# Attention with a Mish MLP: the second-mask value products as quarter tiles, with the sums of a pair in two PSUM banks

## The chip, the cores and the metric

One core of a Trainium2 chip runs the whole kernel. The metric is the device time of one execution in microseconds, the median of three runs. One execution was also profiled; its trace is what the rows below come from. TensorE does the matrix products, VectorE, ScalarE and GpSimd the elementwise work, and SyncE (SP) issues the DMAs. In the views they are PE (PEld for its weight loads), DVE, ACT, POOL and SP.

## What is computed

Eight batches, eight heads, 576 positions, head size 64, all in fp32. Attention is causal with a window of 128 keys; its output, laid out as 4608 rows of 512, goes through an MLP with a Mish activation.

```python
scores = scale * np.matmul(q, k.transpose(0, 1, 3, 2))
rel = pos[:, None] - pos[None, :]
mask = (rel >= 0) & (rel < 128)
scores = np.where(mask, scores + bias, -1e9)
attn = np.exp(scores - scores.max(-1)); attn = attn / (attn.sum(-1) + 1e-9)
x = np.matmul(attn, v)                    # (8, 8, 576, 64) -> (4608, 512)
h = x @ w_in                              # 512 -> 2048
g = h * np.tanh(np.log1p(np.exp(h)))
out = g @ w_out                           # 2048 -> 512
```

## The kernel before

**The MLP.** Batches are taken one after another, 512 positions each; the last 64 positions of all batches are collected in DRAM (`xs`) and form a ninth group. For each group `first` (line 756) does the products with `w_in` into PSUM tiles `h`, `mish` the activation, `parts` (line 778) splits the result into a high and a low part, and `second` (line 810) does the products with `w_out` into `po`. High and low parts make three products of reduced-precision fp32 out of one exact one. ScalarE makes the high part by a copy and the low part is the difference; for the activations GpSimd subtracts, for x VectorE does (`x_high`, `x_low`, lines 320 to 326).

**The attention.** Heads are taken in pairs (`p` = 0 to 3), one head on array columns 0 to 63, the other on 64 to 127. The first 512 queries of a pair are two half pairs (`unit`, line 328, `half` = 0 and 1) of 256 queries, two blocks of 128 each; the last 64 queries of both heads go together (`last_unit`, line 458). A group of 64 queries sees at most 192 keys: 64 old ones, 64 middle ones that are all in reach, and 64 new ones. The steps of a half pair:

- `scores`: products of queries and keys as quarter tiles of the array (64 rows by 64 columns), four at a time, into two PSUM banks (`s`).
- `exps`: VectorE adds the bias and takes the extreme (`pz`, `mx`), ScalarE the exponential and the sum (`sm`).
- `fold`, `scale`: old and new keys of one query never share a place in the mask, so the new ones are added onto the old ones, and 128 weights remain instead of 192; all are divided by the sum.
- `weights`: TensorE transposes the 128 weights; VectorE multiplies them out of PSUM with two masks (`masks`), so that two versions lie side by side in `pz`.
- `values`: products with the values. The first-mask version is taken with `va`, the second with `vs`, values shifted by 64 positions, or the other way round; all of them over 128 array rows, both heads side by side, into one PSUM bank `o` for both halves of a pair.
- `split_x`: `x_high` and `x_low` of the whole 512 columns.

The last queries' transposes and sums share another bank, tag `w` (`st["t"]`, `pt_0l` to `pt_3l` in the trace), copied out as `xo` and sent to `xs`. The x of pairs 0 to 2 takes the buffers in which their values lie (`load_v`, line 291), so it can be written only when the value products are done.

**The order.** TensorE and SP run in the order in which the program issues; a hand-written list of due times (`times`, lines 447 and 521) says where each step of the attention lies between the products of `second` of the batch before (line 913). VectorE, ScalarE and GpSimd are ordered by a planner, except in the stages marked fixed. From batch 2 on (`b > 1`), the value products of both halves and of the last queries of a pair follow each other, then come the last queries' scores and the two halves' scores of the next pair, in one slot; the transposes of both halves come in two steps some ten products of `second` later. In batch 1 each half has its slot of its own, and GpSimd folds and scales. Batch 0 runs by itself at the start (`first_attention`) while the weights come in.

Of the kernel before, what the change touches and what calls it, by code (L numbers as in the profile page):

```python
# [60 lines left out]
def attention_mish_mlp(  # L61
# [47 lines left out]
    vb = [const.tile([P, P], F32, tag=f"vb{i}", name=f"vb{i}") for i in range(2)]  # L109
    for t in vb:  # L110
        nc.gpsimd.memset(t[64:P], 0.0)


    masks = const.tile([P, 2, P], BF16, tag="masks", name="masks")
    nc.gpsimd.memset(masks, 1.0)
    for r in (slice(0, 64), slice(64, P)):

        nc.gpsimd.affine_select(
            out=masks[:, 0, r], in_=masks[:, 0, r], compare_op=ALU.is_gt, fill=0.0, base=0,
            pattern=[[-1, 64]], channel_multiplier=1,  # L120
        )
        nc.gpsimd.affine_select(
            out=masks[:, 1, r], in_=masks[:, 1, r], compare_op=ALU.is_ge, fill=0.0, base=0,
            pattern=[[1, 64]], channel_multiplier=-1,
        )
# [165 lines left out]
    def load_v(b, p):  # L291
        cs = slice(p * P, (p + 1) * P)

        pl, tag = (xp, f"x{p}") if p < NP - 1 else (at, "v")
        t = pl.tile([P, 2, 4, P], F32, tag=tag, name=f"v{b}_{p}", bufs=1)
        va, vs = t[:, 0], t[:, 1]
        load(va, v[b, 0:CH, cs].rearrange("(k p) d -> p k d", p=P))
        load(vs, v[b, 64:S, cs].rearrange("(k p) d -> p k d", p=P))
        load(vb[p % 2][:64], v[b, CH:S, cs])
        qkv[("v", b, p)] = ((va, vs), vb[p % 2])  # L300
# [19 lines left out]
    def x_high(b, p, o):  # L320
        x = xt[(b, p)] = xp.tile([P, 2, CH], F32R, tag=f"x{p}", name=f"x{b}_{p}")
        act.activation(x[:, 0, :], o, AF.Copy)

    def x_low(b, p, o):
        x = xt[(b, p)]
        dve.tensor_tensor(out=x[:, 1, :], in0=o, in1=x[:, 0, :].bitcast(F32), op=ALU.subtract)

    def unit(b, p, half):
# [8 lines left out]
        name = f"{b}_{p}_{half}"  # L337

# [28 lines left out]
        def fold():  # L367
            sm, pz = st["sm"], st["pz"]
            if b == 1:
                two = pz if half else pz[:, 1:4:2]  # L370
                pool.tensor_tensor(out=two[:, :, :64], in0=two[:, :, :64], in1=two[:, :, P:SPAN], op=ALU.add)
            act.activation(sm, sm, AF.Copy, bias=1e-9)
            dve.reciprocal(sm, sm)

        def scale():
            sm, pz = st["sm"], st["pz"]
            if b == 1:
                pool.tensor_tensor(
                    out=pz[:, :, :P], in0=pz[:, :, :P],
                    in1=sm.rearrange("p (c n) -> p c n", n=1).to_broadcast([P, 4, P]), op=ALU.mult,  # L380
                )
                return

            unread = at.tile([P, 4], F32, tag="un", name=f"un{name}")
            for c in range(4):
                n = 0
                if half or c % 2:
                    n = 64
                    dve.tensor_tensor_reduce(
                        out=pz[:, c, :n], in0=pz[:, c, :n], in1=pz[:, c, P:SPAN], scale=sm[:, c : c + 1],  # L390
                        scalar=3.0e38, op0=ALU.add, op1=ALU.min, accum_out=unread[:, c : c + 1],
                    )
                act.activation(pz[:, c, n:P], pz[:, c, n:P], AF.Copy, scale=sm[:, c : c + 1])

        def weights():
# [3 lines left out]
            for c in range(4):  # L399
                pe.transpose(pt[:, c, :], pz[:, c, :P], ident)  # L400
            if half == 0:
# [7 lines left out]
                in1=masks.rearrange("p u (c n) -> p u c n", c=1).to_broadcast([P, 2, n, P]),  # L409
# [12 lines left out]
        def pieces(t, c0, count, step):  # L422
            if step == 64:
                return t[:, c0 : c0 + 64 * count]
            return t.rearrange("p (k n) -> p k n", n=64)[:, c0 // 64 : (c0 + step * (count - 1)) // 64 + 1 : step // 64, :]

        def values():
            va = qkv[("v", b, p)][0]
            if half == 0:
                qkv[("o", b, p)] = ps.tile([P, 512], F32, tag="o", name=f"o{b}_{p}")  # L430
            o = qkv[("o", b, p)]
            for n, (vu, kb, c0, count, step, oc) in enumerate(prods):
                for i in range(2):
                    pf = st["pz"][:, 2 * i : 2 * i + 2, :].rearrange("p a n -> p (a n)")
                    pe.matmul(
                        pieces(o[HEAD[i]], oc, count, step), lhsT=va[vu][:, kb, HEAD[i]],
                        rhs=pieces(pf, c0, count, step),
                        start=(half == 0 and n == 0), stop=(half == 1 and n == len(prods) - 1),
                        skip_group_check=True,
                    )  # L440
# [13 lines left out]
        return list(zip(times, (  # L454
            scores, lambda: exps(0), lambda: exps(1), fold, scale, weights, values, split_x,
        )))

    def last_unit(b, p):
# [27 lines left out]
        def fold():  # L486
# [3 lines left out]
            un = at.tile([P, 1], F32, tag="unl", name=f"un{name}")  # L490
# [6 lines left out]
        def weights():  # L497
            t = st["t"] = ps.tile([P, 512], F32, tag="w", name=f"pt{name}")
# [5 lines left out]
                in1=masks[:, :, :64].rearrange("p u (i n) -> p u i n", i=1).to_broadcast(shape),  # L504
# [3 lines left out]
        def values():  # L508
            va, vl = qkv[("v", b, p)]
            o = st["t"][:, P : P + LEFT]  # L510
            for n, val in enumerate((va[0][:, 3, :], vl)):
                for i in range(2):
                    pe.matmul(
                        o[HEAD[i]], lhsT=val[:, HEAD[i]], rhs=st["pf"][:, n, i, :],
                        start=(n == 0), stop=(n == 1), skip_group_check=True,
                    )
# [4 lines left out]
        times = (-0.001, 0.5, 0.9, 1.4, 1.995)  # L521
        if b > 1:
            times = (-0.01, 0.21, 0.5, 1.78 if p == 1 else 1.7, 1.98)
        return list(zip(times, (scores, exps, fold, weights, values)))
# [458 lines left out]
```

## Time and profile before

| what | value |
|---|---|
| median of three runs | 975.83 us (974.78 to 976.23) |
| span of the profiled execution | 973.1 us |
| instructions in the trace | 17500 |
| TensorE matmul busy | 962.8 us, 99%, 6660 records |
| TensorE weight loads busy | 788.4 us, 81% |
| VectorE, ScalarE, GpSimd busy | 351.9 us (36%), 454.4 us (47%), 260.1 us (27%) |
| traffic to and from HBM | 56.49 MB read, 10.49 MB written, 69 GB/s |

The span runs from the first to the last instruction; what lies around it is the rest of the device time. Matmul records overlap, since each is shown from its start to its last result, so what one costs is read from the distance of starts rather than from its own duration. Every fp32 product of the attention is two passes, and each pass is one record. Times in the rows are microseconds from the start of the span, with two decimals.

### The profile page before, as it was taken

What the parts mean: (1) busy time and instruction counts of PE and PEld (TensorE: products, weight loads), DVE (VectorE), ACT (ScalarE), POOL (GpSimd) and SP (SyncE); (2) the same over time, 40 slices, a digit from 0 to 9 for tenths busy, and PEclk for the clock granted to TensorE, in tenths of its full rate; (3) what the DMA queues carried; (4) which work ended last, traced back from release to release, by engine and by line L of the source; (5) the groups of instructions that cost most, each with busy time, mean ns of one, the idle gap of its engine ahead of it and who ended that gap; (6) DMA issues with size and microseconds to landing.
All of it is one profiled execution on the core that took longest, in us unless ns stands there. A gap on an engine that the chain in (4) does not pass through costs nothing.

```text
span 973.1 us, 17500 instructions
## 1 busy us (share of the span) xinstructions
PE 962.8 (99%) x6660; PEld 788.4 (81%) x6660; DVE 351.9 (36%) x1430; ACT 454.4 (47%) x1256; POOL 260.1 (27%) x238
## 2 busy tenths in 40 slices
PE   9899999999999999999999999999999999999998
PEld 7688778888888888888888888888888888888886
DVE  5896861056302660066203750166105640100000
ACT  6798753165425653276315742366316642322121
POOL 5578751023111221032102311032102311241042
PEclk9999999999999999999999999999999999999999
DMA  7993320032102410123002410222003210000001
GB/s 200 357 371 102 98 81 22 1 108 89 50 1 73 120 32 23 46 76 100 24 1 73 123 51 0 73 74 77 24 1 103 69 45 1 22 22 23 1 12 32
DMA packets 70244, 68.12 MB, mean 70 GB/s; under 512 B 14480, under 2 KB 50960, under 8 KB 70160
## 3 DMA queue, kind: packets, MB, share of 16 engines
q1 hardware_dynamic: 69744, 66.67, 21.7%
q8 instruction: 53, 0.87, 0.4%
q10 hardware_dynamic: 416, 0.33, 0.1%
q14 instruction: 31, 0.25, 0.1%
HBM read 56.49 MB, written 10.49 MB: 69 GB/s over the span
## 4 chain that ended last, share of the span: by engine, by line
PE 89%; DMA 5%; POOL 2%; SPq 1%; issue 1%; DVE 1%; ACT 0%; POOLq 0%
PE po L49 39%; PE h L49 36%; PE s L49 8%; PE o L49 5%; DMA wi<-in_moe_w_in_dram 2%; DMA wo<-in_moe_w_out_dram 2%; POOL so L49 1%; SPq L49 1%; POOL gg L49 1%; DVE pz L49 1%; PE warm L49 1%; PE pt_0l L49 0%; DMA qk<-in_k_dram 0%; PE pt_2l L49 0%; PE pt_1l L49 0%
## 5 line engine op out<-in xcount | busy, mean ns | idle before, releaser
L49 PE MATMUL po<-so,gg 128*128 128x512 f32 x1728 | 420.8, 396 | 0.0
L49 PE MATMUL h<-x,si 128*128 128x512 f32 x1728 | 393.3, 389 | 0.0
L49 PEld LDWEIGHTS h<-x,si 128*128 128x128 f32 x1728 | 324.2, 188 | 67.4
L49 PEld LDWEIGHTS po<-so,gg 128*128 128x128 f32 x1728 | 317.0, 188 | 71.7 <-issue 8.9
L49 POOL TENSOR_TENSOR gg<-g,gg 128x512 fp32r<-128x512 f32 x144 | 186.2, 1294 | 653.6 <-ACT gg L49 653.5
L49 DVE CUSTOM_DVE_ANT_0 pz<-s,nb 128x192 f32<-128x192 f32 (+1 forms) x308 | 92.1, 328 | 299.5 <-PE s L49 296.9
L49 ACT ACTIVATE g<-h 128x1024 f32<-128x1024 f32 x72 | 74.1, 1030 | 255.5 <-PE h L49 255.5
L49 ACT ACTIVATE pz<-pz,mx 128x192 f32<-128x192 f32 (+1 forms) x256 | 110.9, 434 | 42.1 <-DVE mx L49 40.2
L49 ACT ACTIVATE gg<-g 128x512 fp32r<-128x512 f32 x144 | 89.8, 625 | 73.0 <-PE po L49 69.2
L49 DVE COPY ob<-po 128x512 f32<-128x512 f32 x18 | 12.3, 686 | 126.0 <-PE po L49 126.0
L49 PEld LDWEIGHTS o<-pz,v 128*64 128x64 f32 x1120 | 45.7, 137 | 13.2 <-DVE pz L49 8.5
L49 ACT ACTIVATE x<-o 128x512 fp32r<-128x512 f32 x32 | 19.1, 596 | 79.1 <-PE o L49 34.9
L49 DVE CUSTOM_DVE_ANT_0 pz<-pz,sm 128x64 f32<-128x64 f32 x144 | 55.5, 433 | 1.3
L49 DVE TENSOR_TENSOR pz<-s,masks 128x512 f32<-128x512 f32 (+1 forms) x56 | 52.5, 946 | 4.7 <-PE s L49 4.7
L49 ACT ACTIVATE pz<-pz,sm 128x128 f32<-128x128 f32 (+1 forms) x192 | 53.2, 348 | 0.1
L49 PE MATMUL o<-pz,v 128*64 128x64 f32 (+2 forms) x1120 | 51.2, 245 | 0.1
L49 ACT ACTIVATION_READ_ACCUMULATOR pz<-pz,mx 128x1 f32 x256 | 47.8, 187 | 0.0
L49 PE MATMUL s<-ident,pz 128*128 128x128 f32 (+1 forms) x280 | 41.4, 274 | 0.9 <-POOL pz L49 0.9
L49 PEld LDWEIGHTS s<-ident,pz 128*128 128x128 f32 (+1 forms) x280 | 33.6, 138 | 9.9 <-POOL pz L49 1.8
L49 PE MATMUL s<-qk 64*64 64x192 f32 (+1 forms) x896 | 40.8, 316 | 0.0
L49 ACT ACTIVATE ob<-po 128x512 f32<-128x512 f32 x18 | 10.8, 598 | 52.0 <-PE po L49 52.0
L49 PEld LDWEIGHTS s<-qk 64*64 64x64 f32 x896 | 28.7, 132 | 4.8 <-issue 0.4
(159 smaller groups left out, 528.2 us busy)
## 6 DMA issues: line engine op xcount, KB each, us to landing
v<-in_v_dram SPq DMA_DIRECT2D x56, 256.0 KB, 3.7
wi<-in_moe_w_in_dram SPq DMA_DIRECT2D x16, 512.0 KB, 10.7
wo<-in_moe_w_out_dram SPq DMA_DIRECT2D x16, 512.0 KB, 10.2
out_dram<-ob SPq DMA_DIRECT2D x32, 256.0 KB, 2.0
qk<-in_q_dram SPq DMA_DIRECT2D x28, 288.0 KB, 3.1
qk<-in_k_dram SPq DMA_DIRECT2D x28, 288.0 KB, 3.6
first<-in_v_dram SPq DMA_DIRECT2D x4, 256.0 KB, 3.8
vs<-in_v_dram SPq DMA_DIRECT2D x4, 256.0 KB, 3.8
```

The source lines that it names most:

```text
L49: ins = method(*args, **kwargs)
```

## The change

The half pairs keep their 128 folded weights, but in the second half the fold now lies behind the middle keys: the new keys' place takes the sum (`both`), and the weights that are transposed are columns 64 to 191 (`folded`). So in the first half the keys that need the second mask lie in array rows 0 to 63, in the second half in rows 64 to 127. The mask tile has a third plane for that. Products with the first version stay over 128 rows. Products with the second version, whose other half would be zeros, are taken over their 64 rows only, as quarter tiles; so is the last queries' product with `vl`, for which `vb` shrinks to 64 rows. They are kept in `late` and issued together by `late_values`, one of the first half (rows 0 to 63) after one of the second (rows 64 to 127), for both heads. The first half's sums go into the last queries' bank, the second half's into `o`, so the two row halves write to different banks. x is split in two pieces of 256 columns. From batch 2 on the late products of a pair come right behind the next pair's last-query scores; in batch 1 each half has its own late step.

```diff
-    masks = const.tile([P, 2, P], BF16, tag="masks", name="masks")
+    vb = [const.tile([64, P], F32, tag=f"vb{i}", name=f"vb{i}") for i in range(2)]
+    masks = const.tile([P, 3, P], BF16, tag="masks", name="masks")
     nc.gpsimd.memset(masks, 1.0)
+    for plane, base, sign, op in ((0, 0, 1, ALU.is_gt), (1, 0, -1, ALU.is_ge), (2, 64, -1, ALU.is_ge)):
+        for r in (slice(0, 64), slice(64, P)):
+            nc.gpsimd.affine_select(
+                out=masks[:, plane, r], in_=masks[:, plane, r], compare_op=op, fill=0.0, base=base,
+                pattern=[[-sign, 64]], channel_multiplier=sign,
+            )
     for r in (slice(0, 64), slice(64, P)):
+        nc.gpsimd.memset(masks[64:P, 1, r], 1.0)
         nc.gpsimd.affine_select(
-            out=masks[:, 0, r], in_=masks[:, 0, r], compare_op=ALU.is_gt, fill=0.0, base=0,
+            out=masks[64:P, 1, r], in_=masks[64:P, 1, r], compare_op=ALU.is_gt, fill=0.0, base=0,
...
+    def x_high(b, p, o, n0=0):
+        if n0 == 0:
+            xt[(b, p)] = xp.tile([P, 2, CH], F32R, tag=f"x{p}", name=f"x{b}_{p}")
+        act.activation(xt[(b, p)][:, 0, n0 : n0 + o.shape[-1]], o, AF.Copy)
+
+    def x_low(b, p, o, n0=0):
+        high, low = (xt[(b, p)][:, k, n0 : n0 + o.shape[-1]] for k in range(2))
+        dve.tensor_tensor(out=low, in0=o, in1=high.bitcast(F32), op=ALU.subtract)
+
+    late = {}
+
+    def late_values(b, p):
+        parts = late.pop((b, p))
+        for n in range(max(len(part) for part in parts)):
+            for i in range(2):
+                for part in parts:
+                    if n < len(part):
+                        o, val, w = part[n](i)
+                        pe.matmul(o, lhsT=val, rhs=w, start=False, stop=n == len(part) - 1, skip_group_check=True)
...
+        both, folded = (slice(P, SPAN), slice(64, SPAN)) if half else (slice(0, 64), slice(0, P))
...
-                pe.transpose(pt[:, c, :], pz[:, c, :P], ident)
+                pe.transpose(pt[:, c, :], pz[:, c, folded], ident)
...
         if half == 0:
-            prods = [(0, 0, 128, 3, 64, 0), (1, 0, 320, 1, 64, 192), (0, 1, 384, 1, 64, 128), (1, 1, 448, 1, 64, 192)]
+            prods = [(0, 0, P, SPAN, 0), (1, 0, 320, 64, SPAN)]
+            rest = [(0, 1, 384, P), (1, 1, 448, SPAN)]
         else:
-            prods = [
-                (0, 1, 0, 1, 64, 256), (1, 1, 64, 1, 64, 320), (0, 2, 128, 2, 128, 256),
-                (1, 2, 192, 2, 128, 320), (0, 3, 384, 1, 64, 384), (1, 3, 448, 1, 64, 448),
-            ]
+            prods = [(1, 1, 128, 64, 0), (0, 2, 192, 64, 64), (1, 2, 384, 64, 128), (0, 3, 448, 64, SPAN)]
+            rest = [(1, 0, 0, 0), (0, 1, 64, 64), (1, 1, 256, 128), (0, 2, 320, SPAN)]
...
             if half == 0:
-                qkv[("o", b, p)] = ps.tile([P, 512], F32, tag="o", name=f"o{b}_{p}")
-            o = qkv[("o", b, p)]
+                o = qkv[("t", b, p)][:, SPAN : SPAN + 256]
+                qkv[("o", b, p)] = [o]
+            else:
+                o = ps.tile([P, 512], F32, tag="o", name=f"o{b}_{p}")[:, :256]
+                qkv[("o", b, p)].append(o)
...
+            def work(vu, kb, c0, oc):
+                return lambda i: (
+                    o[HEAD[i], oc : oc + 64], va[vu][HALF[half], kb, HEAD[i]], pf[i][HALF[half], c0 : c0 + 64]
+                )
+
+            late.setdefault((b, p), [[], []])[half] += [work(*x) for x in rest]
...
                 for part in (x_high, x_low):
-                    part(b, p, qkv[("o", b, p)])
-
-        times = (0, 0.02, 0.25, 0.7, 0.95, 1.3, 1.99, 2.02)
+                    for u, o in enumerate(qkv[("o", b, p)]):
+                        part(b, p, o, 256 * u)
+
+        def late_half():
+            if b == 1 or half == 1:
+                late_values(b, p)
+
+        times = (0, 0.02, 0.25, 0.7, 0.95, 1.3, 1.99, 2.02, 1.9995)
...
-                (-1, -0.8, -0.7, -0.3, -0.25, 0.7 if p == 1 else 0.65, 0.97, 0.99) if half
-                else (0, 0.02, 0.12, 0.4, 0.45, 1.4 if p == 1 else 1.3, 1.96, 1.96)
+                (-1, -0.8, -0.7, -0.3, -0.25, 0.7 if p == 1 else 0.65, 0.97, 0.996, 0.995) if half
+                else (0, 0.02, 0.12, 0.4, 0.45, 1.4 if p == 1 else 1.3, 1.96, 1.96, 1.96)
...
-            for n, val in enumerate((va[0][:, 3, :], vl)):
-                for i in range(2):
-                    pe.matmul(
-                        o[HEAD[i]], lhsT=val[:, HEAD[i]], rhs=st["pf"][:, n, i, :],
-                        start=(n == 0), stop=(n == 1), skip_group_check=True,
-                    )
+            for i in range(2):
+                pe.matmul(
+                    o[HEAD[i]], lhsT=va[0][:, 3, HEAD[i]], rhs=st["pf"][:, 0, i, :],
+                    start=False, stop=False, skip_group_check=True,
+                )
+            late[(b, p)][0].append(lambda i: (o[HEAD[i]], vl[:, HEAD[i]], st["pf"][:64, 1, i, :]))
```

## Rows read from the trace of the kernel before

**Rows 1.** The page: busy time by engine, and the chain that ended last.

```profile
PE 962.8 (99%) x6660; PEld 788.4 (81%) x6660; DVE 351.9 (36%) x1430; ACT 454.4 (47%) x1256; POOL 260.1 (27%) x238
...
PE 89%; DMA 5%; POOL 2%; SPq 1%; issue 1%; DVE 1%; ACT 0%; POOLq 0%
```

**Rows 2.** Stretches: start and end, us, busy (instructions) by engine, clock, DMA.

```profile
core 0: us, PE busy (x) PEld busy (x) DVE busy (x) ACT busy (x) POOL busy (x), PEclk, DMA share, GB/s
195.32:258.92 63.60, 63.60 (x582) 52.01 (x581) 39.19 (x182) 39.15 (x140) 16.91 (x13) 1.00 0.28 84
```

**Rows 3.** Timeline of TensorE, one pair's slot in batch 2: start, us, instruction, records.

```profile
210.60 1.80 PE L49 MATMUL o<-pz,v 128*64 128x192 f32 x40
212.23 0.29 PE L49 MATMUL pt_0l<-pf_0l,v 128*64 128x64 f32 x4
212.35 0.29 PE L49 MATMUL pt_0l<-pf_0l,vb 128*64 128x64 f32 x4
212.46 0.50 PE L49 MATMUL s<-qk,qd 128*64 128x96 f32 x8
212.90 1.42 PE L49 MATMUL s<-qk 64*64 64x128 f32 x32
214.25 0.50 PE L49 MATMUL po<-so,gg 128*128 128x512 f32 x1
```

**Rows 4.** Timeline of TensorE in batch 0: products over 64 rows, both heads.

```profile
24.05 0.33 PE L49 MATMUL o<-pz,first 64*64 64x64 f32 x4
24.22 0.28 PE L49 MATMUL o<-pz,vs 64*64 64x64 f32 x4
24.34 0.28 PE L49 MATMUL o<-pz,first 64*64 64x64 f32 x4
```

**Rows 5.** Timeline of TensorE in batch 0: value products (two start at 19.83) beside score products.

```profile
19.83 0.22 PE L49 MATMUL o<-pz,vs 64*64 64x64 f32 x1
19.83 0.37 PE L49 MATMUL s<-first 64*64 64x192 f32 x1
...
19.84 0.37 PE L49 MATMUL s<-first 64*64 64x192 f32 x1
```

**Rows 6.** Timelines of VectorE and TensorE at the transposes, pairs 1 and 2.

```profile
222.54 0.28 DVE L49 CUSTOM_DVE_ANT_0 pz<-pz,sm 128x64 f32<-128x64 f32 x1
...
223.01 0.60 PE L49 MATMUL s<-ident,pz 128*128 128x128 f32 x4
...
236.68 0.28 DVE L49 CUSTOM_DVE_ANT_0 pz<-pz,sm 128x64 f32<-128x64 f32 x1
...
237.46 0.60 PE L49 MATMUL s<-ident,pz 128*128 128x128 f32 x4
```

**Rows 7.** Timelines of ScalarE and VectorE: splitting x, and copies of 256 columns.

```profile
212.56 0.60 ACT L49 ACTIVATE x<-o 128x512 fp32r<-128x512 f32 x1 [3.11 <-PE pt_0l L49]
...
213.19 0.69 DVE L49 TENSOR_TENSOR x<-o,x 128x512 fp32r<-128x512 f32 x1 [0.29 <-ACT x L49]
213.80 0.27 DVE L49 CUSTOM_DVE_ANT_0 pz<-s,nb 64x128 f32<-64x128 f32 x1
...
222.74 0.41 DVE L49 COPY pz<-s 128x256 f32<-128x256 f32 x1
...
18.40 0.36 ACT L49 ACTIVATE pz<-s 64x256 f32<-64x256 f32 x1
```

**Rows 8.** Timelines of VectorE and TensorE in batch 1.

```profile
125.48 1.22 DVE L49 TENSOR_TENSOR pz<-s,masks 128x1024 f32<-128x1024 f32 x1
...
126.75 1.12 PE L49 MATMUL o<-pz,v 128*64 128x64 f32 x24
...
116.78 0.88 PE L49 MATMUL s<-qk 64*64 64x192 f32 x16
...
117.52 0.69 DVE L49 TENSOR_TENSOR x<-o,x 128x512 fp32r<-128x512 f32 x1 [0.49 <-ACT x L49]
```

**Rows 9.** Timeline of GpSimd at the start of the kernel.

```profile
8.11 0.23 POOL L49 TENSOR_SCALAR sm<-sm 128x4 f32<-128x4 f32 x1 [4.71 <-ACT pz L49]
```

More of the change, by code (lines that the diff above doesn't have):

```diff
@@ L370, in fold @@
                 two = pz if half else pz[:, 1:4:2]
-                pool.tensor_tensor(out=two[:, :, :64], in0=two[:, :, :64], in1=two[:, :, P:SPAN], op=ALU.add)
+                pool.tensor_tensor(out=two[:, :, both], in0=two[:, :, :64], in1=two[:, :, P:SPAN], op=ALU.add)
             act.activation(sm, sm, AF.Copy, bias=1e-9)
@@ L378, in scale @@
                 pool.tensor_tensor(
-                    out=pz[:, :, :P], in0=pz[:, :, :P],
+                    out=pz[:, :, folded], in0=pz[:, :, folded],
                     in1=sm.rearrange("p (c n) -> p c n", n=1).to_broadcast([P, 4, P]), op=ALU.mult,
@@ L382, in scale @@
                 return
-            unread = at.tile([P, 4], F32, tag="un", name=f"un{name}")
+            unread = at.tile([P, 4], F32, tag="un", name=f"un{name}", bufs=1)
             for c in range(4):
@@ L389, in scale @@
                     dve.tensor_tensor_reduce(
-                        out=pz[:, c, :n], in0=pz[:, c, :n], in1=pz[:, c, P:SPAN], scale=sm[:, c : c + 1],
+                        out=pz[:, c, both], in0=pz[:, c, :n], in1=pz[:, c, P:SPAN], scale=sm[:, c : c + 1],
                         scalar=3.0e38, op0=ALU.add, op1=ALU.min, accum_out=unread[:, c : c + 1],
@@ L408, in weights @@
                 in0=pt.rearrange("p (u c) n -> p u c n", u=1).to_broadcast([P, 2, n, P]),
-                in1=masks.rearrange("p u (c n) -> p u c n", c=1).to_broadcast([P, 2, n, P]),
+                in1=masks[:, half : half + 2].rearrange("p u (c n) -> p u c n", c=1).to_broadcast([P, 2, n, P]),
                 op=ALU.mult,
@@ L429, in values @@
             if half == 0:
-                qkv[("o", b, p)] = ps.tile([P, 512], F32, tag="o", name=f"o{b}_{p}")
-            o = qkv[("o", b, p)]
-            for n, (vu, kb, c0, count, step, oc) in enumerate(prods):
+                o = qkv[("t", b, p)][:, SPAN : SPAN + 256]
[3 more added lines that the diff above has]
+                qkv[("o", b, p)].append(o)
+            pf = [st["pz"][:, 2 * i : 2 * i + 2, :].rearrange("p a n -> p (a n)") for i in range(2)]
+            for n, (vu, kb, c0, count, oc) in enumerate(prods):
                 for i in range(2):
-                    pf = st["pz"][:, 2 * i : 2 * i + 2, :].rearrange("p a n -> p (a n)")
                     pe.matmul(
[L436 to L439, printed above, removed]
-                    )
+                        o[HEAD[i], oc : oc + count], lhsT=va[vu][:, kb, HEAD[i]],
+                        rhs=pf[i][:, c0 : c0 + count], start=n == 0, stop=False, skip_group_check=True,
+                    )
+            def work(vu, kb, c0, oc):
[3 more added lines that the diff above has]
+            late.setdefault((b, p), [[], []])[half] += [work(*x) for x in rest]
         def split_x():
@@ L489, in fold @@
             dve.reciprocal(sm, sm)
-            un = at.tile([P, 1], F32, tag="unl", name=f"un{name}")
+            un = at.tile([P, 1], F32, tag="unl", name=f"un{name}", bufs=1)
             dve.tensor_tensor_reduce(
@@ L497, in weights @@
         def weights():
-            t = st["t"] = ps.tile([P, 512], F32, tag="w", name=f"pt{name}")
+            t = st["t"] = qkv[("t", b, p)] = ps.tile([P, 512], F32, tag="w", name=f"pt{name}")
             pe.transpose(t[:, :P], st["pz"][:, :P], ident)
@@ L503, in weights @@
                 out=pf, in0=t[:, :P].rearrange("p (u i n) -> p u i n", u=1, i=2).to_broadcast(shape),
-                in1=masks[:, :, :64].rearrange("p u (i n) -> p u i n", i=1).to_broadcast(shape),
+                in1=masks[:, :2, :64].rearrange("p u (i n) -> p u i n", i=1).to_broadcast(shape),
                 op=ALU.mult,
@@ L509, in values, with keep @@
             va, vl = qkv[("v", b, p)]
[L510 to L516 removed]
+            o = st["o"] = st["t"][:, P : P + LEFT]
+            for i in range(2):
[4 more added lines that the diff above has]
+            late[(b, p)][0].append(lambda i: (o[HEAD[i]], vl[:, HEAD[i]], st["pf"][:64, 1, i, :]))
+        def keep():
+            o = st["o"]
             xo = at.tile([P, LEFT], F32, tag="xo", name=f"xo{name}", bufs=5)
@@ L519, in values @@
             sp.dma_start(out=xs[p, :, b * LEFT : (b + 1) * LEFT], in_=xo)
-        times = (-0.001, 0.5, 0.9, 1.4, 1.995)
+        times = (-0.001, 0.5, 0.9, 1.4, 1.995, 1.9996)
         if b > 1:
-            times = (-0.01, 0.21, 0.5, 1.78 if p == 1 else 1.7, 1.98)
-        return list(zip(times, (scores, exps, fold, weights, values)))
+            times = (-0.01, 0.21, 0.5, 1.78 if p == 1 else 1.7, 1.98, 1.9955)
+        return list(zip(times, (scores, exps, fold, weights, values, keep)))
     def first_attention():
```

20 lines of the change are left out of this document (2 added, 18 removed).

## The prediction, made before the changed kernel ran

> **What bounds the kernel now.** I read the page first for which engine is full and which work the chain runs through [rows 1]: TensorE is busy 99% of 973.1 us and holds 89% of the chain; the other three stand at 47% or less. The median of the runs, 975.83 us, lies 2.7 us over this span; I take that as unchanged and make the sum on the span.
>
> Then the table of stretches: from batch 2 on, every batch has one phase of 63.60 us in which the second matmul of the MLP is interleaved with the attention of the next batch; there are six of them, all of 63.60, with TensorE busy throughout at a granted clock of 1.00, which is the level of 2.4 GHz [rows 2] (the first of the six). There the change acts. A group of TensorE instructions taken out is therefore time gained, unless something that was just in time for TensorE now comes late. So two readings are needed: what a product costs on TensorE (its timeline), and how early its inputs are (the timelines of VectorE and ScalarE beside it).
>
> **Price of a product.** In one pair's slot [rows 3] every fp32 product is two passes, and the two heads run side by side on the two column halves, so a product pair is four records. 64 columns: 212.23 to 212.35 to 212.46 is 0.115 us, 0.058 a pass. The 40 records from 210.60 to 212.23 are, by the code, 14 such passes (0.81), 4 of 128 columns, 2 of 192 and about 0.05 for starting: the 0.77 left over 896 columns is 0.86 ns a column, so 0.11 for 128 and 0.163 for 192. A change of array form has two parts: the pause (212.46 to 212.90 is 0.44 for four passes of 96 columns, 0.33 by this price, so 0.11), and a slow first pass (24.05 to 24.22 is 0.17 for what then takes 0.115, so 0.05) [rows 3, 4]; together 0.15. Rows 4 also show that a product over 64 rows, alone on its half, takes the same 0.115: halving rows gains nothing by itself; only running both row halves together does.
>
> Does that happen? The scores do it: 32 records in quarter tiles, four at a time, 2 passes of 128 and 6 of 192 columns, are 1.20 by the price of two tiles, with pause and start 1.35; the rows say 214.25 - 212.90 = 1.35 [rows 3]. Four cost what two cost. That is at 128 and 192 columns; at 64 no row has all four with 64 columns, but at 19.83 two 64-column products of the value matmul start with two score products, all four within 0.02 us [rows 5]. So for a pass of four I take 0.058; bounds are 0.058 and 0.115 (taking turns).
> The Trainium skill speaks against this in "TensorE: Matmul & The Clock Gate", section "Wait — 56ns, not 53.3ns?": starts are said never to come closer than about 25 ns, however short the product. By that a pass of four would take an estimated 0.10 us. The trace differs, with four starts in 0.02 us [rows 5]; it is weighed below as a rival.
>
> **Part by part, a pair of batches 2 to 7.** Leaving the full-row stream: first half 2 products of 64 columns (4 passes, 0.23); second half the 4 passes of 128 columns where 64-column passes stay (0.44); the last queries 1 product (2 passes, 0.12). Sum 0.79. Coming in: 7 products for each head, 4 from rows 64 to 127 and 3 from rows 0 to 63, in 4 steps of two passes, 8 x 0.058 = 0.46. Net -0.32 us of TensorE a pair. The form changes cost nothing in pairs 0 to 2: the quarter tiles are put behind the next pair's last-query scores and right ahead of its block scores, which are quarter tiles already, so the pause only comes earlier. After pair 3 no scores follow: one more form change, +0.15.
>
> **What TensorE then waits for.** Call T the start of the value products (210.60). Sums are split into x by ScalarE and VectorE, now as two pieces each. Before, ScalarE's copy began at T + 1.96, released by the last-query products, since x takes the buffer of the values [rows 7]. Now: first half 0.49, second half to 0.96, last queries to 1.07, scores of the last queries with the pause to 1.51, last quarter pass at 1.97 with 0.22 of its own [rows 5] and about 0.05 to be seen: ScalarE begins at T + 2.24, 0.28 later. Its first piece takes 0.36 (a 256-column copy from PSUM), and VectorE's two pieces follow after 0.03. No row has such a piece: half of the 0.61 between the whole one and the next instruction is 0.30, the 128x256 copy takes 0.41 [rows 7]; I take 0.35. So VectorE reaches the next pair's first bias at 2.24 + 0.36 + 0.03 + 0.70 = T + 3.33, against 3.20 before (213.80): the softmax chain starts 0.13 later (bounds +0.03 and +0.25), while TensorE arrives at that pair's transposes 0.32 earlier.
>
> How much room is there? The transposes of the second half wait for VectorE's last fold. In pair 1 it ends at 222.82 and they start at 223.01: 0.19; in pair 2 at 236.96 against 237.46: 0.50 [rows 6]. Pair 3 is like pair 1; pair 0's chain starts ahead of any value products of its phase and is untouched. A wait that really is one shows 0.05 between VectorE's end and TensorE's start (126.70 to 126.75 [rows 8]), so the rooms are 0.14 and 0.45.
> - Pairs 0 to 1, and 2 to 3: the chain rules; -0.14 + 0.13 = -0.01 each.
> - Pairs 1 to 2: -0.32 wanted; 0.32 + 0.13 just fills 0.45; -0.32.
> - After pair 3: -0.32 + 0.15 = -0.17; x is wanted by the next first matmul only behind twelve products of the second one and nine of its own, so nothing waits.
>
> Sum -0.51 a batch, six batches -3.1 us.
>
> **Batch 1** runs its halves in different slots, so only two tiles run together, and rows 4 price them like the old ones. First half: as many passes as before. Second half: 4 passes of 0.11 become 8 of 0.058, +0.03, four pairs +0.12. Pair 3 changes form once more in both slots, +0.30. Together +0.4. Its product sums now hold the bank of the transposes until x is split; the next user comes some 2 us later, so I cost that at nothing (up to +0.3 a pair if x is late).
>
> **Costed at nothing.** The added memsets and selections for the masks run on GpSimd, which sits idle 4.71 us before its first work at 8.11 [rows 9]; without that cover they would be about 1 us. Folding the middle keys first moves the same elements through the same instructions. The copy of the last queries and its DMA on SP's queue come about as late as before, ahead of the same loads; `load_v` behind it is for a pair two slots on. Batch 0 keeps its products.
>
> Forecast: 975.83 - 3.1 + 0.4 = 973.2 us. With VectorE's pieces at 0.30 the chain is only 0.03 later and a batch gives -0.71: 972.0. At 0.41 it is 0.25 later; pairs 1 to 2 then keep only -0.20 and a batch gives -0.15: 975.4.
>
> **Rivals.**
> - Biases go ahead of the split. VectorE's order is the planner's, and the first scores are there at about T + 2.5, before the split can begin at 2.63. If a bias fills that gap the chain starts no later, and at best nothing waits: 6 x (4 x -0.32 + 0.15) + 0.4 = -6.4, 969.5; with half of the waits left, 971.3. For it: VectorE would stand idle otherwise. Against: in batch 1 scores begun at 116.78 were there by about 117.2, and the bias still stood behind the split begun at 117.52 [rows 8].
> - The chain eats all. If the split comes out some 0.30 later, pairs 0 to 1 and 2 to 3 lose 0.16 each, pairs 1 to 2 keep 0.15, and the +0.4 of batch 1 is about all that is left: 975.8 to 976.3.
> - Slower: the row halves take turns. 14 passes instead of 8, +0.35 a pair, and the split that much later: +0.34, +0.03, +0.34, +0.18 a batch, with batch 1 +5.7: 981.6. It decides from 0.11 us a pair, passes of 0.072 instead of 0.058. Against it stand the scores and rows 5; for it, that those rows have no four 64-column products.
> - Slower, starts are spaced: six passes of four at 0.10 instead of 0.058, +0.25 a pair; the same steps give +0.24, -0.07, +0.24, +0.08 a batch, +3.3 with batch 1: 979.2. Rows 5 speak against it directly. This is what the Trainium skill's section named above would make of it, as an estimate.
>
> **How the numbers follow.** About 0.2% (1.95 us) is what a measurement of this kernel can tell from no change, so faster means below 973.9. Forecast 0.45, of which 0.30 lies below that and 0.15 between; biases ahead 0.27, faster; chain eats all 0.13, same; turns 0.10 and spaced starts 0.05, slower. Faster 0.57, same 0.28, slower 0.15. The range takes the first three cases, 969.5 to 976.3, and leaves 0.15 above.
>
> **What would show it.** In the changed trace: 14 quarter-tile products a pair, in 28 records, taking about 0.5 us from first to last before the scores of the next pair (0.87 if they take turns); the phase of 63.60 at about 63.1 (62.5 with no wait, 64.5 with turns); transposes of the second half in pairs 1 and 3 starting 0.05 after VectorE's last fold, in pairs 0 and 2 later; VectorE's first bias near T + 3.33; batch 1's phase 0.4 longer. I am wrong if the planner sets the split or the copies of the MLP elsewhere, or if one of VectorE's folds meets GpSimd's subtraction where it now passes.

## The result, and the profile after

The changed kernel takes 985.01 us (median of 4 runs, 983.39 to 987.71), the kernel before beside it 975.31 us: a ratio of 1.0104 with an interval of 1.0085 to 1.0123. It is 1% slower, where 973.2 was predicted, and outside the range. The page of after, its busy times and the chain that ended last:

```profile
span 983.4 us, 18006 instructions
...
PE 960.3 (98%) x6884; PEld 782.8 (80%) x6884; DVE 353.6 (36%) x1458; ACT 456.3 (46%) x1284; POOL 260.4 (26%) x242
...
PE 69%; DVE 14%; ACT 10%; issue 3%; POOL 2%; DMA 0%; SPq 0%; POOLq 0%; ACTq 0%; DVEq 0%
```

TensorE has less work (960.3 us busy, 962.8 before) in a longer span, and its share of the chain falls from 89% to 69% [rows 1]; VectorE and ScalarE now hold 24%. This points to work that was taken off TensorE, and to something that it waits for and that came late. The table of stretches gives the place, the same phase of batch 2 as in [rows 2] (start and end, us, busy and instructions by engine, clock, DMA), and below it what TensorE waited for there (what waits, on what, us in total, times, longest):

```profile
196.76:261.77 65.01, 62.95 (x613) 50.95 (x612) 39.38 (x186) 39.37 (x144) 16.88 (x13) 1.00 0.28 83
```

```profile
PE pt_1l L49 <- DVE pf_1l L49: 1.1, 1, 1.1
PE pt_3l L49 <- DVE pf_3l L49: 0.5, 1, 0.5
PE pt_2l L49 <- DVE pf_2l L49: 0.3, 1, 0.3
```

The phase of 63.60 us is 65.01, and TensorE is idle in it for 2.06 us. Pair 0 is late too, by 0.21; that is too little for the list and shows in the starts (see "Why the prediction was wrong"). The waiting instructions are the first half's value products. Here is pair 1's slot on TensorE and VectorE's work ahead of it (start, us, instruction, records, idle time before it):

```profile
225.62 1.09 PE L49 MATMUL po<-so,gg 128*128 128x512 f32 x4
227.82 0.66 PE L49 MATMUL pt_1l<-pz,v 128*64 128x192 f32 x8 [1.11 <-DVE pf_1l L49]
228.31 0.64 PE L49 MATMUL o<-pz,v 128*64 128x64 f32 x16
228.77 0.29 PE L49 MATMUL pt_1l<-pf_1l,v 128*64 128x64 f32 x4
228.89 0.50 PE L49 MATMUL s<-qk,qd 128*64 128x96 f32 x8
229.32 0.27 PE L49 MATMUL pt_1l<-pz,v 64*64 64x64 f32 x1
229.33 0.27 PE L49 MATMUL o<-pz,v 64*64 64x64 f32 x1
229.34 0.27 PE L49 MATMUL pt_1l<-pz,v 64*64 64x64 f32 x1
229.34 0.27 PE L49 MATMUL o<-pz,v 64*64 64x64 f32 x1
229.43 0.22 PE L49 MATMUL pt_1l<-pz,v 64*64 64x64 f32 x1
...
229.49 0.22 PE L49 MATMUL pt_1l<-pz,v 64*64 64x64 f32 x1
```

```profile
225.03 0.68 DVE L49 TENSOR_TENSOR pz<-s,masks 128x512 f32<-128x512 f32 x1
225.62 0.68 DVE L49 COPY ob<-po 128x512 f32<-128x512 f32 x1
226.22 1.21 DVE L49 TENSOR_TENSOR pz<-s,masks 128x1024 f32<-128x1024 f32 x1
227.35 0.41 DVE L49 TENSOR_TENSOR pf_1l<-pt_1l,masks 128x256 f32<-128x256 f32 x1
```

Read the second block first. The first half's weights (`pz`, 128x512) are masked by 225.71. Before, its products needed no more than that. Now they write into the last queries' tile `pt_1l`, and they start 0.06 us after the last multiply of the queue, the one that reads that tile, has ended (227.76). Ahead of that multiply stand the copy of the MLP's output and the second half's multiply. The products write columns 192 to 447 and the multiply reads columns 0 to 127: they share a tile and a bank, but no data.

Theory W, then: the time is lost to the wait of the first half's products for the last queries' mask multiply, because both now use one tile. Its rivals: the quarter tiles themselves are dear (Q), or the split of x in two pieces is late (X). The ratios of the experiments are to the kernel before as it ran beside them (medians 974.70 to 974.82). To compare kernels I use the period, the mean time from one batch's first matmul to the next in batches 1 to 7 (six intervals, from TensorE's timeline):

| kernel | period, us | time, us |
|---|---|---|
| before | 107.12 | 975.3 |
| changed | 108.56 | 985.0 |
| e1_bank_only | 108.59 | 983.6 |
| e2_own_bank | 108.34 | 988.4 |
| e3_turns | 109.17 | 994.3 |
| e4_swap | 107.35 | 976.8 |
| e5_roles | 107.10 | 975.2 |
| e6_low_late / e7_roles_low_late / e8_before_low_late | 108.53 / 107.15 / 107.12 | 984.2 / 975.1 / 974.5 |
| e10_roles_bias_first | 106.31 | 970.3 |
| e11_roles_ob_act | 106.50 | 971.0 |
| e12_both | 105.97 | 969.1 |
| e13_both_turns | 106.68 | 972.5 |
| e14_after_order | 106.90 | 973.5 |
| c2_before_order | 107.12 | 974.5 |

One thing stands beside the periods: in some executions TensorE's granted clock is at its lower level for some us at the start of the first MLP (0.56 on average from 40 to 43 us in the profile of after, 1.00 in that of before), which costs about 1.6 us (the first interval, ahead of the six, is 112.94 in after and 111.30 in e6, which has after's period and kept its clock) and lies in the 983.4 of after.

### The profile page after: what moved, and what is told of

It is laid out like the page before. It is cut to its first block, busy times and chain, and to the rows that moved or that the text cites. A ratio compares the mean times of both kernels' runs of the same rounds, so it can differ in the third digit from the quotient of the medians.

```text
span 983.4 us, 18006 instructions
## 1 busy us (share of the span) xinstructions
PE 960.3 (98%) x6884; PEld 782.8 (80%) x6884; DVE 353.6 (36%) x1458; ACT 456.3 (46%) x1284; POOL 260.4 (26%) x242
## 4 chain that ended last, share of the span: by engine, by line
PE 69%; DVE 14%; ACT 10%; issue 3%; POOL 2%; DMA 0%; SPq 0%; POOLq 0%; ACTq 0%; DVEq 0%
PE h L49 39%; PE po L49 19%; DVE pz L49 10%; ACT pz L49 8%; PE s L49 4%; PE o L49 3%; DVE x L49 1%; POOL so L49 1%; PE pt_2l L49 1%; PE pt_0l L49 1%; PE pt_1l L49 1%; PE pt_3l L49 1%; POOL gg L49 1%; ACT x L49 1%; ACT gg L49 0%
## 5 line engine op out<-in xcount | busy, mean ns | idle before, releaser
L49 ACT ACTIVATE x<-o 128x256 fp32r<-128x256 f32 (+1 forms) x32 | 13.1, 409 | 93.3 <-PE o L49 93.3
L49 PE MATMUL o<-pz,v 128*64 128x64 f32 (+1 forms) x896 | 37.0, 223 | 0.2
L49 PEld LDWEIGHTS s<-qk 64*64 64x64 f32 x896 | 32.2, 133 | 1.4 <-issue 0.4
L49 PEld LDWEIGHTS o<-pz,v 128*64 128x64 f32 (+1 forms) x896 | 30.9, 136 | 2.2 <-DVE pz L49 1.9
```

Source lines behind the costliest of these rows:

```text
L49: ins = method(*args, **kwargs)
```

## The experiments

**The bank alone (e1).** The kernel before, with only the first half's sums moved into the last queries' tile and x split in two; no quarter tiles.

```
             if half == 0:
-                qkv[("o", b, p)] = ps.tile([P, 512], F32, tag="o", name=f"o{b}_{p}")
-            o = qkv[("o", b, p)]
+                o = qkv[("t", b, p)][:, SPAN : SPAN + 256]
+                qkv[("o", b, p)] = [o]
+            else:
+                o = ps.tile([P, 512], F32, tag="o", name=f"o{b}_{p}")[:, :256]
+                qkv[("o", b, p)].append(o)
...
```

> The kernel before with one part of the change alone: the first half's sums go into the last queries' bank and x is split in two pieces; all value products stay over 128 rows, none is a quarter tile. Theory W (the first product into that bank has to wait until VectorE has read the last queries' transposed weights out of it, pt to pf): in the trace of before that read ends 0.15 to 0.76 us behind the start of the products in every pair of batches 2 to 7, and the chain to it is tied to the pair before; worked through the four pairs that is +0.21, +0.82, +0.21, +0.22 a batch, six batches +8.7 us, so about 984 us, with the waits of the value products named pt <- DVE pf. Rival Q (the quarter tiles or their changes of form cost the time): no more than 1 us from before, about 975.5 us, and no such wait.

Measured 983.57 us, ratio 1.0098 (1.0072 to 1.0124). The whole loss is there without one quarter tile, so Q falls. X is not yet apart from W, but TensorE's waits name W alone (batches 2 to 7):

```profile
PE pt_1l L49 <- DVE pf_1l L49: 4.2, 6, 0.8
PE pt_3l L49 <- DVE pf_3l L49: 0.6, 3, 0.2
```

The list leaves out short waits and comes to 4.8 us. By the starts the first value product of the four pairs is late by 0.21, 0.79, 0.21 and 0.21 in batch 2, 1.42 together, against 1.47 of period (108.59 - 107.12): the loss lies at the heads of the slots.

**Another bank for the last queries (e2).** The changed kernel, with the last queries' transposes in the second bank of the first half's score tile.

```
+            if half == 0:
+                qkv[("s1", b, p)] = t[:, 1, :]
...
+                qkv[("t", b, p)] = ps.tile([P, 512], F32, tag="w", name=f"oa{b}_{p}")
...
-            t = st["t"] = qkv[("t", b, p)] = ps.tile([P, 512], F32, tag="w", name=f"pt{name}")
+            t = qkv.pop(("s1", b, p))
...
```

> The changed kernel with one edit: the last queries' transposed weights go into the second score bank of the pair's first half, which is idle by then, so the first half's sums have their bank for themselves. Theory W: the wait is gone and what is left is the forecast's own sum, -0.5 us a batch and +0.4 for batch 1: 972.6 us (970 to 975), second phases of 63.1 us. Rival Q: about 984 us as before this edit.

Measured 988.39, ratio 1.0140 (1.0124 to 1.0156): a miss. The wait for `pf` is gone, but a new one stands in its place, of the same kind. Waits of batches 2 to 7, and one of them in TensorE's timeline:

```profile
PE s L49 <- DVE pz L49: 8.4, 18, 0.5
```

```profile
232.40 0.33 PE L49 MATMUL s<-ident,pz_1l 128*128 128x128 f32 x1 [0.54 <-DVE pz L49]
```

The last queries' transpose, into bank 1, waits until VectorE has read the first half's weights out of bank 0 of the same tile (in this trace that multiply ends at 232.34). The transpose's own input had been ready since 229.88. So to share a tile is enough for the wait, even where the banks differ; whether two uses of one bank would wait without a common tile, no run shows. Batch 1 lost some 5 us more to waits for VectorE (4.8 in TensorE's list, which the changed kernel does not have).

**Two tiles at a time (e3).** As e2, with all of the first half's late products ahead of all of the second half's.

```
-        for n in range(max(len(part) for part in parts)):
-            for i in range(2):
-                for part in parts:
+        for part in parts:
+            for n in range(len(part)):
+                for i in range(2):
...
```

> As e2_own_bank, but the quarter-tile products of the first half are all issued before those of the second half, so that only two tiles run together. If the four-tile order is what pays: the late products take 14 passes of 0.058 us instead of 8, 0.35 us more a pair on TensorE; with the softmax chain that much later 1.4 us a batch, about 8 us over e2_own_bank, 981 us. If TensorE has no other work in the way and the chain has room it is at least the 0.35 for pairs 1 to 2 and the last one, +4 us. Rival (the tiles of two row halves take turns anyway, or TensorE reorders them): the same as e2_own_bank within 1 us.

Measured 994.34, ratio 1.0208 (1.0184 to 1.0232), 6.0 over e2, between the 4 and the 8 of the expectation. Four tiles at a time are worth something; how much can't be read from a kernel that waits (e13 repeats it in one that doesn't).

**The second half's products first (e4).** The changed kernel, with its order in the slot turned round.

```
-                else (0, 0.02, 0.12, 0.4, 0.45, 1.4 if p == 1 else 1.3, 1.96, 1.96, 1.96)
+                else (0, 0.02, 0.12, 0.4, 0.45, 1.4 if p == 1 else 1.3, 1.975, 1.975, 1.975)
```

> The changed kernel with the second half's full-row products ahead of the first half's, from batch 2 on. Nothing is taken away; the products into the shared bank only start 0.52 us later in the slot, behind products that do not touch it. Theory W: of the waits of 0.2, 1.2, 0.4 and 0.6 us in the four pairs 0.52 is covered in each, only pair 1 keeps one of about 0.6: 974 to 976 us. Rival Q: as the changed kernel, about 984 us.

Measured 976.82, ratio 1.0022 (1.0012 to 1.0031), 0.8 above the range. The wait for `pf` is gone; now the second half's own multiply is late at the head of the slot:

```profile
PE o L49 <- DVE pz L49: 5.7, 12, 0.8
```

**The two tiles exchanged (e5).** The sums of the first half and of the last queries go into the tile `o`, those of the second half, which come second, into the last queries' tile.

```
             if half == 0:
-                o = qkv[("t", b, p)][:, SPAN : SPAN + 256]
+                t = ps.tile([P, 512], F32, tag="o", name=f"o{b}_{p}")
+                o, qkv[("l", b, p)] = t[:, :256], t[:, 256 : 256 + LEFT]
...
             else:
-                o = ps.tile([P, 512], F32, tag="o", name=f"o{b}_{p}")[:, :256]
+                o = qkv[("t", b, p)][:, SPAN : SPAN + 256]
...
-            o = st["o"] = st["t"][:, P : P + LEFT]
+            o = st["o"] = qkv.pop(("l", b, p))
```

> The changed kernel with the two banks exchanged: the first half's and the last queries' sums go into the bank that nothing else uses, the second half's into the bank of the last queries' transposed weights. The wait on that read then meets the second half's products, 0.49 us behind the start of the slot. Theory W (the wait goes with the tile that is read): no wait in pairs 0, 2 and 3; pair 1 keeps one, its chain reaches the read's end 15.35 us behind the pair before, so +0.47 us there against before, with -0.32, -0.01 and -0.17 for the rest: about even per batch, 974 to 977 us. Rival (what waits is any product behind that read, whatever its tile): as the changed kernel, 984 us.

Measured 975.24, ratio 1.0007 (0.9998 to 1.0016). Now the first half's products, 0.5 us of TensorE, cover `pf`, except in pair 1, where the copy of the MLP's output stands ahead of it:

```profile
PE pt_1l L49 <- DVE pf_1l L49: 3.2, 6, 0.5
```

So the kernel is as fast as before: what the quarter tiles take off TensorE goes into waits, these 3.2 us and more that the list leaves out (see e10 and e11). Since x is still split in two, at the same place, X falls as the main cause.

**Low part of x later (e6, e7, e8).** The subtraction for x was given a later time in the changed kernel (e6), in e5 (e7) and in the kernel before (e8), to let the next pair's biases go first.

```
+        def split_low():
+            if half == 1:
+                for u, o in enumerate(qkv[("o", b, p)]):
+                    x_low(b, p, o, 256 * u)
...
-                (-1, -0.8, -0.7, -0.3, -0.25, 0.7 if p == 1 else 0.65, 0.97, 0.996, 0.995) if half
+                (-1, -0.8, -0.7, -0.3, -0.25, 0.7 if p == 1 else 0.65, 0.97, 0.996, 0.995, 0.996 if p == 3 else 1.5) if half
...
```

> The changed kernel with VectorE's two subtractions of the x split put later for pairs 0 to 2, into the gap that VectorE has behind the first half's folds; the banks stay. Theory (the softmax chain behind the split sets when the read ends): biases start about 0.75 us earlier behind the value products, so the waits of pairs 2 and 3 go and pair 1 keeps about 0.2, pair 0 its 0.2, which no split precedes: -0.4 us a batch, 972 to 975 us. Rival (the chain does not matter, the wait is one of order on TensorE): 984 us.

> Banks exchanged as in e5_roles and the subtractions later as in e6_low_late. By theory W and the chain nothing waits any more, so what the quarter tiles take off TensorE shows: -0.32 us in each pair and +0.15 for the form change behind the last, -1.1 us a batch, six batches -6.5, batch 1 +0.4: 969 us (968 to 971). Rival (four quarter tiles do not pay at 64 columns, or the form changes eat it): 975 us or more.

> Control: the kernel before with VectorE's subtraction of the x split later for pairs 0 to 2, and nothing else. Before, TensorE waits for none of this, so by theory the time is that of before within 0.5 us, about 975 us. If the later subtraction is itself the gain of e6 and e7 it is faster by some us.

Measured 984.2, 975.1 and 974.46 (ratios 1.0100, 1.0007 and 0.9997), as fast as the kernels they were made from: two misses and a control, for one reason. VectorE's instructions stand in the same sequence as before the edit in each of the three; the planner sets it, and the due time only moves the statement. These three say nothing of W or X.

**The order forced (e10), the copy moved (e11), both (e12).** From e5: biases and the low part of x in an order written out; the copy of the MLP's output in the first half of the phase on ScalarE.

```
+    def dve_in_order(work):
+        dve.fixed = True
+        work()
+        dve.fixed = False
...
-            scores, lambda: exps(0), lambda: exps(1), fold, scale, weights, values, split_x, late_half,
+            scores, lambda: dve_in_order(lambda: exps(0)) if b > 1 else exps(0),
+            lambda: dve_in_order(lambda: exps(1)) if b > 1 else exps(1), fold, scale, weights, values, split_x, late_half, lambda: dve_in_order(split_low) if b > 1 else split_low(),
...
```

```
-            if t == 0:
+            if t == 0 and (half or not 0 < c < B - 1):
                 dve.tensor_copy(ob, po[t])
```

> The exchanged banks, and VectorE's order written out so that the next pair's first biases stand ahead of both low parts of x (about 0.7 us of VectorE at every pair's head). Theory W (the last queries' mask multiply at the end of VectorE's queue is the one wait left, 0.5 us in pair 1 of each batch): everything behind the biases comes up to 0.6 us earlier, the multiply ends ahead of the slot, the 3.2 us of waiting in batches 2 to 7 go, and the time is 975.2 - 3.2 = 972.0 us (971.5 to 972.8). Rival: the biases are not what sets the multiply's time, because the copies of the MLP output (0.68 us) and ScalarE's exponentials lie between; then the wait stays at 0.4 us or more in pair 1 and the time is 974.5 to 975.3.

> The exchanged banks, and the copy of the MLP output (128x512, 0.68 us, which stands ahead of the second half's mask multiply in pair 1) given to ScalarE. Theory W: the two multiplies behind it end 0.6 us earlier, the wait of 0.5 us in pair 1 goes, nothing else is late: 975.2 - 3.2 = 972.0 us (971.5 to 972.8). Rival: ScalarE is itself in the chain, and what it does after the copy (the high part of g, the scaling of the weights) comes 0.6 us late, so that TensorE waits there instead: 974 to 976.

> Both of the foregoing changes. Theory W: the wait is gone with either of them and TensorE has nothing else to wait for, so that both together bring no more than one: 972.0 us (971.3 to 972.8). Rival: a second wait behind the first (transposes for the fold, 0.1 us in pairs 1 and 3) still costs, and both together bring a further 0.2 us a batch or more: 970.8 or less.

Measured 970.33 (ratio 0.9949, 0.9936 to 0.9962), 971.00 (0.9957, 0.9944 to 0.9970) and 969.08 (0.9937, 0.9924 to 0.9949). All three lie below their ranges. Each of the first two takes the wait off the list, and gains more than the 3.2 us that the list gave it: from start to start the second half's products were held by 0.70 a batch and not 0.53 (1.19 us behind the first half's in e5, 0.49 in e12), and the transposes of pairs 1 and 3 and the second half's products of pair 3 had been late by about 0.1 each; with 0.70 this is 1.0 of the 1.13 us of period between e5 and e12. Both together gain a further 1.3 us by the medians and 0.34 us a batch by the periods. The rival's mark was 0.2: it was right, and W's "no more than one" was not. e12 is faster than the kernel before and the changed one. Its phase of batch 2, and pair 1 on TensorE and VectorE:

```profile
195.33:257.79 62.46, 62.46 (x614) 50.92 (x612) 38.99 (x185) 39.97 (x145) 16.91 (x13) 1.00 0.29 86
```

```profile
223.65 1.32 PE L49 MATMUL po<-so,gg 128*128 128x512 f32 x5
224.90 0.66 PE L49 MATMUL o<-pz,v 128*64 128x192 f32 x8
225.39 0.64 PE L49 MATMUL pt_1l<-pz,v 128*64 128x64 f32 x16
...
226.40 0.27 PE L49 MATMUL o<-pz,v 64*64 64x64 f32 x1
226.41 0.27 PE L49 MATMUL pt_1l<-pz,v 64*64 64x64 f32 x1
226.42 0.27 PE L49 MATMUL o<-pz,v 64*64 64x64 f32 x1
226.42 0.27 PE L49 MATMUL pt_1l<-pz,v 64*64 64x64 f32 x1
```

```profile
222.87 1.87 DVE L49 TENSOR_TENSOR pz<-s,masks 128x512 f32<-128x512 f32 x2
224.65 0.41 DVE L49 TENSOR_TENSOR pf_1l<-pt_1l,masks 128x256 f32<-128x256 f32 x1
...
227.70 0.28 DVE L49 CUSTOM_DVE_ANT_0 pz<-s,nb 64x128 f32<-64x128 f32 x1 [0.45 <-PE s L49]
```

TensorE is busy through all 62.46 us, and starts on the products with no idle time. `pf_1l` ends at 225.06, 0.16 behind the slot's head, but 0.33 ahead of the products that need it (225.39). The next pair's first bias comes 2.80 us after the head (227.70 - 224.90), where it was 3.33 in the changed kernel, with the split ahead of it (next section).

**Is it the order, or the quarter tiles (c2)?** The kernel before, with e12's two changes of VectorE's work.

> The kernel before (no quarter tiles, its own banks) with the two changes of VectorE's work alone: biases ahead of the low part of x, and the copy of the MLP output of the first half given to ScalarE. Theory W (the kernel before waits for nothing there, so earlier multiplies bring it nothing, and the gain of the best version is the quarter tiles'): 974.8 us (974.0 to 975.6). Rival (the order itself gains, whatever TensorE does): 970 to 972.

Measured 974.46, ratio 0.9996 (0.9987 to 1.0006), period unchanged. The order by itself brings nothing; the 5.4 us between this kernel and e12 come with the quarter tiles and the two tiles for their sums.

**Two tiles at a time, with nothing waiting (e13).** e12 with e3's edit.

> The best version (exchanged banks, both changes of VectorE's work) with the late products in two blocks, the first half's all before the second half's, so that two tiles run at a time and not four. It does the same products with no wait in the way. By the pass of 0.058 us, 18 passes in place of 10 cost 8 x 0.058 = 0.46 us a pair: 4 x 0.46 = 1.9 us in each of six batches = 11 us, and the time is 980. By the 6 us that the same edit cost in the kernel with banks of their own: 975. Rival (tiles of two products in turn overlap anyway): 969 to 971.

Measured 972.47, ratio 0.9974 (0.9965 to 0.9984): 3.4 us over e12, a miss below both figures. The phase, and the late products of pair 1 in TensorE's timeline:

```profile
198.70:261.86 63.16, 63.16 (x614) 51.57 (x613) 39.01 (x185) 39.97 (x145) 16.92 (x13) 1.00 0.29 85
```

```profile
229.93 0.39 PE L49 MATMUL o<-pz,v 64*64 64x64 f32 x6
230.11 0.27 PE L49 MATMUL pt_1l<-pz,v 64*64 64x64 f32 x2
...
230.28 0.33 PE L49 MATMUL pt_1l<-pz,v 64*64 64x64 f32 x5
230.40 0.32 PE L49 MATMUL s<-qk 64*64 64x128 f32 x1
...
230.56 0.22 PE L49 MATMUL pt_1l<-pz,v 64*64 64x64 f32 x2
```

0.70 a phase, 0.175 a pair. The 0.46 of the expectation rests on a miscount of mine: it is 14 passes for 8, 0.35, as the prediction has it; half of that is measured. The rows show why: in program order all twelve records of the first half (eight of `pz`, four of the last queries) stand ahead of the second half's, yet the second half's products (`pt_1l`) begin after six of them, and the next scores (230.40) begin ahead of the last of these (230.56). The row halves overlap even when they are issued in blocks. By the periods the same edit cost 0.83 a batch in e3 (109.17 - 108.34) and 0.71 here; what the other 0.12 is stays open.

**The order without the exchange (e14).** The changed kernel's tiles, e12's VectorE.

> The changed kernel with its banks as they are, and the two changes of VectorE's work. Theory W: the first half's products still wait for the last queries' multiply, which now ends some 0.16 to 0.2 us behind the slot's head in every pair (as it does in the best version, where the second half's products cover it), and reach TensorE some 0.06 us later: 0.2 to 0.25 us a pair, 0.8 to 1.0 a batch, 5 to 6 us over the best version: 974 to 975, equal to the kernel before. Rival (order alone mends the changed kernel): 969 to 970.5.

Measured 973.54, ratio 0.9981 (0.9969 to 0.9993), half a us under the range. The wait shrinks to what W says of it, and stays:

```profile
PE pt_2l L49 <- DVE pf_2l L49: 0.9, 6, 0.2
PE pt_1l L49 <- DVE pf_1l L49: 0.9, 6, 0.2
PE pt_3l L49 <- DVE pf_3l L49: 0.9, 6, 0.2
```

It costs 0.93 us of period against e12 (106.90 and 105.97), some 0.2 at the head of each slot. By the periods the change of order alone takes 1.66 us a batch from the changed kernel, the exchange a further 0.93; the medians fall by 11.5 and 4.5 us, but the first figure also holds the lower clock that some of the changed kernel's runs had.

## Why the prediction was wrong, point by point

- **What bounds the kernel: right.** TensorE was full, and work taken from it is time, once nothing waits (e12, c2).
- **Price of the quarter tiles: right.** Passes of four step by 0.06 (229.43 to 229.49) and the four starts lie within 0.02 us (229.32 to 229.34), so spaced starts did not come. The Trainium skill's "TensorE: Matmul & The Clock Gate", section "Wait — 56ns, not 53.3ns?", has about 25 ns between starts; the trace does not agree where the products go to different tiles, and the measurement decides. The net on TensorE a batch, with no waits, is 4 x -0.32 + 0.15 = -1.13 by the prediction and 105.97 - 107.12 = -1.15 by e12.
- **The chain from the split to the first bias: right.** T + 3.33 was forecast; in batch 2 of after T is 212.41 and the bias starts at 215.74, by 2.24 + 0.42 + 0.67 where the sum has 2.24 + 0.39 + 0.70. Here are ScalarE's and VectorE's rows behind pair 0, to be read against [rows 7]:

```profile
214.65 0.38 ACT L49 ACTIVATE x<-o 128x256 fp32r<-128x256 f32 x1 [3.60 <-PE o L49]
...
215.07 0.42 DVE L49 TENSOR_TENSOR x<-o,x 128x256 fp32r<-128x256 f32 x1 [0.30 <-ACT x L49]
215.41 0.41 DVE L49 TENSOR_TENSOR x<-pt_0l,x 128x256 fp32r<-128x256 f32 x1
215.74 0.27 DVE L49 CUSTOM_DVE_ANT_0 pz<-s,nb 64x128 f32<-64x128 f32 x1
```

- **Batch 1: right** where no lower clock confuses it: its interval is 111.29 in e12 and 110.92 before, +0.37 for +0.4.
- **The step that failed** is the cost of the shared bank, and with it the start of the slot, T, which was taken as given. The prediction speaks of it in one sentence, for batch 1 ("the next user comes some 2 us later, so I cost that at nothing (up to +0.3 a pair if x is late)"); for batches 2 to 7 it has no term at all, and no reason why. The sentence asks when the bank comes free for its next user and not what its new user must wait for when it begins. The sums were moved into a tile that VectorE is still reading, so the slot's first product waits for the last of VectorE's four steps ahead of it. In batch 2, by the gap between the starts of the sixth `po` product and the first value product (0.327 before; 0.537, 1.505, 0.704 and 0.902 after), that is 0.21 + 1.18 + 0.38 + 0.57 = 2.34 us. With TensorE's -1.15 and about 0.2 more at the second half's transposes of pairs 1 and 3 it makes +1.39; the phase shows +1.41. Six batches and batch 1 make some 8.8 us; the profiled spans differ by 10.3, of which 1.6 is the lower clock.
- **The trace of before had shown it.** The multiply that reads the tile ended after the products had begun, by 0.15 us in pair 0 (210.75, with the products at 210.60 [rows 3]) and by 0.77 in pair 1 (225.82, with the products at 225.05). There the two used different tiles, and it cost nothing:

```profile
210.34 0.41 DVE L49 TENSOR_TENSOR pf_0l<-pt_0l,masks 128x256 f32<-128x256 f32 x1
...
225.41 0.41 DVE L49 TENSOR_TENSOR pf_1l<-pt_1l,masks 128x256 f32<-128x256 f32 x1
...
225.05 1.80 PE L49 MATMUL o<-pz,v 128*64 128x192 f32 x40
```

- **Why pair 1 is the worst.** It was the latest already before the change, and ahead of its multiply stands a copy of the MLP's output (0.68 us). The list of what would prove me wrong named these copies, but for being moved, and this one had not moved. In the kernel with exchanged tiles, the list shows no wait in any pair once that copy is taken from VectorE (e11). A slot that begins late also starts the next pair's biases late, so the wait can feed itself; VectorE's and ScalarE's shares of the chain fit that, but no run separates this part.
- **Rivals.** Biases ahead of the split gave 969.5 at best; e12, which makes that order, measures 969.1. Row halves that take turns, priced at 0.35 a pair, did not come: the four starts lie within 0.02 us. Even issued in blocks they cost only 0.175 (e13).

## What to carry to other kernels

When results are moved into a buffer that is already in use, ask for both ends of the sharing: who waits for it to come free, and what its first writer must now wait for. In these runs that wait came with the tile, so results that are written early in a slot belong with a buffer whose last reader is early in its queue, and the ones written last may share with the latest. A gain on the full engine shows only when the engines that feed it have the slack for it; here some 0.2 us of waiting a pair was enough to lose 0.93 of the 1.15 us a batch (e14 against e12).

## What the runs showed of the hardware that was not expected

Products on different row halves overlap across the program order: issued in blocks of two tiles, the second block started after six of twelve records of the first, and four tiles in turn were only 0.175 us a pair better (e13). TensorE's clock fell to its lower level (1.2 GHz; 0.50 to 0.63 of full speed from 40 to 43 us) in the profiles of the changed kernel, e2, e4, e7 and e13, and stayed at 1.00 there in the others. In the changed kernel TensorE had been idle for 0.81 us shortly before, and for just as long in the kernel before, where the clock held; on what it hangs stays open. In e2 it fell once more (0.50 from 112 to 115 us), behind idle times of 0.46 and 1.21 us. In e13 the low stretch is longer (0.50 from 43 to 45.5 us as well), and a wait of 1.66 us stands ahead of it. The next profile line is e13's.

```profile
40.00:43.00 3.00, 2.31 (x12) 1.53 (x13) 1.96 (x5) 2.98 (x6) 1.30 (x1) 0.50 1.06 388
```
